# First q norms taken as TensorE columns of squares, and a new order of the first products (attention over channels, then a three-way maxout layer)

## The chip, the cores and the metric

One core of one Trainium2 chip. The metric is the device time of one execution in microseconds (us); a profile of one execution gives the time of every instruction. TensorE is PE in the profile, its weight loads are PEld, VectorE is DVE, ScalarE is ACT, GpSimd is POOL, SyncE is SP.

## The reference, cut to what matters

```python
def _attn_ref(q, k, v, tau):                       # each 4 x 6144 x 256
    qn = q / (np.linalg.norm(q, axis=1, keepdims=True) + 1e-06)
    kn = k / (np.linalg.norm(k, axis=1, keepdims=True) + 1e-06)
    s = kn.transpose(0, 2, 1) @ qn / tau           # 256 x 256 for each batch
    s = s - s.max(-1, keepdims=True)
    a = np.exp(s)
    a /= a.sum(-1, keepdims=True) + 1e-09
    return (v @ a).astype(np.float32)

def _moe_ref(x, w1, w2, w3, w_out):                # x: 24576 x 256, w: 256 x 768
    h = np.maximum(np.maximum(x @ w1, x @ w2), x @ w3)
    return (h @ w_out).astype(np.float32)
```

The kernel multiplies the softmax matrix into the three weights (`aw` = a times w), so that v times `aw` gives h directly. For the first batch nothing can be done before all of q and k are there. Only this first batch is touched by the change; the later ones are prepared beside running work. The tokens of a batch are worked through in chunks of 512, of which chunk 0 and chunk 1 are the first two.

Names in the profile: `gram` is the product of q and k, `e_in` the same after scaling, `et` its exp, `rs_ps` the row sums of `et` and `rinv` their reciprocals; `ew_ps` are the products of `et` with a weight, which are scaled into `aw_sb` (an "evacuation": a copy out of PSUM, the memory that the matmuls write to); `vt` is v transposed. A "piece" of q is what one load brings, 8, 4 or 2 of its 48 groups of 128 tokens.

## The kernel before

The parts that matter, with cuts marked `...`. The q norm comes from the diagonal of q times q, formed beside the gram matrix of q and k:

```python
        for tp in range(NG // 2):
            ...
            for j in range(CC):
                PE.matmul(ps[j][:, 0:C], lhsT=qt[:, tsl, jsl], rhs=kt[:, tsl, :], ...)
                PE.matmul(ps[j][:, C:C + P], lhsT=qt[:, tsl, jsl], rhs=qt[:, tsl, jsl], ...)
    ...
    def softmax_t(ps, rkb):
        for j in range(CC):          # DVE: the diagonal of q*q, by a product with the identity and a sum
            DVE.tensor_tensor_reduce(out=scr, in0=ps[j][:, C:C + P], in1=ident, ...
                                     accum_out=n2q[:, j:j + 1])
        ACT.activation(out=lnq, in_=n2q, func=AF.Ln)
        ACT.activation(out=rq, in_=lnq, func=AF.Exp, scale=-0.5, bias=neg_ln_tau)
        return exp_t(scaled(...), rq)
```

Then six warm-up matmuls, the transposes of the first v on TensorE, and the first part of `aw`: all three weights' products before the first h matmul.

```python
    ps = gram(0)
    for i in range(6):
        PE.matmul(warm_ps, lhsT=ident, rhs=warm, start=(i == 0), stop=(i == 5))
    et = softmax_t(*ps)
    v_transpose_pe(0)
    aw = alloc_aw()
    rinv = aw_first(et, aw)          # products of weights 0, 1, 2; row sums; scaled into aw
    v_transpose(1)                   # by a DMA transpose, for chunk 1
```

## Time and profile before

| what | us |
|---|---|
| time, median of 4 runs (lowest to highest) | 573.54 (573.29 to 574.51) |
| span of the profiled execution | 571.6 |
| last piece of q has landed | 33.75 |
| first exp of the softmax starts | 35.46 |
| first h matmul starts | 37.65 |
| first h matmul of chunk 1 starts | 48.175 |
| transpose of the second v: input landed, result landed | 44.36, 48.07 |

All but the first two rows are moments from the start of the span. A landing is read from the trace's records of a transfer's semaphore: sixteen increments for each transfer (the page counts 16 DMA engines), of which the last is the landing. A "hole" below is a pause of TensorE: the distance between the starts of two matmuls less the pace that matmuls of the size of the first keep when nothing stops them (0.216 us for 512 columns, 0.163 for 384, 0.109 for 256), counted from 0.02 us on.

### The profile page before, as it was taken

What the parts mean: (1) busy time and instruction counts of PE and PEld (TensorE: products, weight loads), DVE (VectorE), ACT (ScalarE), POOL (GpSimd) and SP (SyncE); (2) the same over time, 40 slices, a digit from 0 to 9 for tenths busy, and PEclk for the clock granted to TensorE, in tenths of its full rate; (3) what the DMA queues carried; (4) which work ended last, traced back from release to release, by engine and by line L of the source; (5) the groups of instructions that cost most, each with busy time, mean ns of one, the idle gap of its engine ahead of it and who ended that gap; (6) DMA issues with size and microseconds to landing.
All of it is one profiled execution on the core that took longest, in us unless ns stands there. A gap on an engine that the chain in (4) does not pass through costs nothing.

```text
span 571.6 us, 9437 instructions
## 1 busy us (share of the span) xinstructions
PE 553.2 (97%) x3343; PEld 329.7 (58%) x3344; DVE 416.1 (73%) x658; ACT 309.5 (54%) x540; POOL 233.4 (41%) x237
## 2 busy tenths in 40 slices
PE   3789999999999999999999999999999999999997
PEld 2665555555755555555575555555575555555566
DVE  0048777877887778777767777777768778778775
ACT  1044567677464576776535467767645444444443
POOL 2441357776450078776560058776750000000000
PEclk9999999999999999999999999999999999999999
DMA  9995999884579168884279339984437233132112
GB/s 144 106 172 95 136 239 133 159 134 110 107 86 182 56 116 154 134 150 104 57 131 151 100 81 138 148 141 101 119 86 155 75 78 107 56 104 63 56 55 76
DMA packets 76960, 65.64 MB, mean 115 GB/s; under 512 B 52464, under 2 KB 62576, under 8 KB 76784
## 3 DMA queue, kind: packets, MB, share of 16 engines
q0 software_dynamic: 19072, 26.48, 38.6%
q1 hardware_dynamic: 57696, 38.41, 24.6%
q8 instruction: 26, 0.43, 0.3%
q14 instruction: 22, 0.18, 0.1%
q10 hardware_dynamic: 144, 0.13, 0.1%
HBM read 78.64 MB, written 25.17 MB: 182 GB/s over the span
## 4 chain that ended last, share of the span: by engine, by line
PE 93%; DMA 5%; POOL 0%; issue 0%; DVE 0%; POOLq 0%
PE h_ps L379 65%; PE o_ps L399 22%; DMA q_sb<-in_q_dram 5%; PE gram L250 3%; PE ew_ps L301 3%; POOL k_sb L99 0%; PE o_ps L424 0%; PE ew_ps L325 0%; PE warm_ps L459 0%; PE vt_ps L362 0%; PE gram L181 0%; DVE ht_sb L385 0%; DVE o_sb L451 0%; PE rs_ps L289 0%; PE gram L183 0%
## 5 line engine op out<-in xcount | busy, mean ns | idle before, releaser
L379 PE MATMUL h_ps<-vt_sb,aw_sb 128*128 128x512 bf16 (+1 forms) x1764 | 406.7, 375 | 0.1
L379 PEld LDWEIGHTS <-aw_sb 128*128 128x128 bf16 x1764 | 171.7, 98 | 161.7 <-DVE aw_sb L307 2.4
L384 DVE TENSOR_TENSOR s_mx<-h_ps,s_mx 128x512 bf16<-128x512 f32 (+1 forms) x294 | 198.9, 676 | 82.0 <-ACT s_mx L383 81.8
L383 ACT ACTIVATE s_mx<-h_ps 128x512 bf16<-128x512 f32 (+1 forms) x294 | 172.4, 586 | 124.1 <-PE h_ps L379 123.1
L385 DVE TENSOR_TENSOR ht_sb<-h_ps,s_mx 128x512 bf16<-128x512 f32 (+1 forms) x294 | 200.3, 681 | 30.6
L209 POOL TENSOR_TENSOR acc<-acc,sq 128x768 f32<-128x768 f32 x88 | 144.2, 1648 | 69.3 <-ACT sq L201 53.3
L399 PE MATMUL o_ps<-wo_sb,ht_sb 128*128 128x256 bf16 x1128 | 153.9, 273 | 0.0
L399 PEld LDWEIGHTS <-ht_sb 128*128 128x128 bf16 x1128 | 110.4, 98 | 52.1
L402 ACT ACTIVATE o_sb<-o_ps 128x512 f32<-128x512 f32 x94 | 56.1, 597 | 83.7 <-PE o_ps L399 83.7
L110 POOL DMA_DIRECT2D v_sb<-in_v_dram x48 | 27.8, 584 | 37.6 <-DMA vt_sb<-v_sb 35.4
L201 ACT ACTIVATE sq<-q_sb 128x768 bf16<-128x768 fp8e4 x48 | 40.5, 844 | 0.0
L201 ACT ACTIVATE sq<-k_sb 128x768 bf16<-128x768 fp8e4 x48 | 40.1, 835 | 0.0
L206 POOL CAST acc<-sq 128x768 f32<-128x768 bf16 x6 | 4.9, 820 | 65.0 <-ACT sq L201 65.0
L102 POOL DMA_DIRECT2D q_sb<-in_q_dram x33 | 18.4, 566 | 4.7 <-DMA v_sb<-in_v_dram 3.9
L169 PE MATMUL kk<-k_sb 128*128 128x256 fp8e4 x48 | 7.5, 338 | 11.8 <-DVE k_sb L155 6.4
L99 POOL DMA_DIRECT2D k_sb<-in_k_dram x29 | 16.1, 557 | 2.8 <-issue 1.1
L250 PE MATMUL gram<-k_sb,q_sb 128*128 128x512 fp8e4 x144 | 16.8, 276 | 0.0
L304 ACT ACTIVATE aw_sb<-ew_ps,rinv 128x384 bf16<-128x384 f32 (+1 forms) x24 | 13.2, 555 | 5.7 <-PE ew_ps L301 4.8
L250 PEld LDWEIGHTS <-q_sb 128*128 128x256 fp8e4 x144 | 15.9, 136 | 0.6
L222 POOL PARTITION_ALL_REDUCE tot<-acc x6 | 10.9, 1858 | 11.8 <-issue 5.9
L301 PE MATMUL ew_ps<-w_sb,et 128*128 128x384 bf16 (+1 forms) x96 | 15.6, 313 | 0.0
L181 PE MATMUL gram<-k_sb,q_sb 128*128 128x512 fp8e4 x48 | 11.4, 331 | 2.8 <-DMA q_sb<-in_q_dram 2.7
(64 smaller groups left out, 113.3 us busy)
## 6 DMA issues: line engine op xcount, KB each, us to landing
out_dram<-o_sb SPq DMA_DIRECT2D x41, 512.0 KB, 2.9
v_sb<-in_v_dram POOLq DMA_DIRECT2D x48, 256.0 KB, 4.1
k_sb<-in_k_dram POOLq DMA_DIRECT2D x24, 192.0 KB, 5.7
q_sb<-in_q_dram POOLq DMA_DIRECT2D x24, 192.0 KB, 7.1
out_dram<-o_sb SPq DMA_DIRECT2D x13, 256.0 KB, 2.0
k_sb<-in_k_dram POOLq DMA_DIRECT2D x5, 256.0 KB, 10.7
w_sb<-in_moe_w_dram POOLq DMA_DIRECT2D x9, 128.0 KB, 5.7
kf<-in_k_dram SPq DMA_DIRECT2D x1, 1024.0 KB, 4.9
```

The source lines that it names most:

```text
L102: POOL.dma_start(out=qk[b][0][:, g0:g0 + w, :], in_=q_r[b][:, g0:g0 + w, :])
L110: POOL.dma_start(out=t, in_=v_r[gi // NCH, gi % NCH])
L201: ACT.activation(out=sq, in_=src, func=AF.Square)
L209: POOL.tensor_tensor(out=acc, in0=acc, in1=sq, op=ALU.add)
L250: PE.matmul(g[:, j * C:(j + 1) * C], lhsT=qt[:, tsl, j * P:(j + 1) * P], rhs=kt[:, tsl, :], start=(tp == 0 and j == 0), stop=(tp == NG // ...
L301: PE.matmul(ew[:, :w], lhsT=et[:, j, ic * P:(ic + 1) * P], rhs=w_sb[m][:, j, fsl], start=(j == 0), stop=(j == CC - 1))
L379: PE.matmul(t.rearrange("p (t n) -> p t n", n=P), lhsT=aw[m][:, ic, fsl], rhs=vt[:, tsl, ic, :], start=(ic == 0), stop=(ic == CC - 1))
L383: ACT.activation(out=s_mx, in_=hp[0], func=AF.Copy)
L384: DVE.tensor_tensor(out=s_mx, in0=hp[1], in1=s_mx, op=ALU.max)
L385: DVE.tensor_tensor(out=ht, in0=hp[2], in1=s_mx, op=ALU.max)
L399: PE.matmul(st["ps"][:, half], lhsT=ht[:, fc, t * P:(t + 1) * P], rhs=wo_sb[:, fc, :], start=(fc == 0), stop=(fc == FC - 1))
L402: ACT.activation(out=st["o"][:, t - 1:t + 1, :].rearrange("p t d -> p (t d)"), in_=st["ps"], func=AF.Copy)
```

## The change

Its intent is to shorten the way from the last piece of q to the first h matmul. It has four parts:

1. While the pieces of q arrive, ACT and DVE square them, and TensorE adds the squares of each channel up by matmuls with a single column of ones. The norm is complete four such matmuls after the last square; the two diagonal reductions on DVE go.
2. Two warm-up matmuls in place of six.
3. The transposed first v is written to two banks of PSUM, so that DVE and ACT can copy it at the same time.
4. The third weight's products, and then the first weight's products of the next part, stand between the matmuls of the first h block.

```diff
+        def squares(g0, w):
+            h = w // 2
+            ...
+            ACT.activation(out=a[:, 0:h, :], in_=ra, func=AF.Square)
+            DVE.tensor_tensor(out=d[:, 0:h, :], in0=rd, in1=rd, op=ALU.mult)
+            return [(t, r) for t in (a, d) for r in range(h)]
+        def columns(rows, first=False, last=False):
+            for n, (t, r) in enumerate(rows):
+                for j in range(CC):
+                    PE.matmul(nq[:, j:j + 1], lhsT=t[:, r, j * P:(j + 1) * P], rhs=ones_c, ...)
 ...
-            DVE.tensor_tensor_reduce(out=scr, in0=ps[j][:, C:C + P], in1=ident, scale=1.0, scalar=0.0,
-                                     op0=ALU.mult, op1=ALU.add, accum_out=n2q[:, j:j + 1])
 ...
-    for i in range(6):
-        PE.matmul(warm_ps, lhsT=ident, rhs=warm, start=(i == 0), stop=(i == 5))
+    for i in range(2):
+        PE.matmul(warm_ps, lhsT=ident, rhs=warm, start=(i == 0), stop=(i == 1))
 ...
+        matmuls(0, range(CC))
+        third(lambda: ACT.activation(out=s_mx, in_=hp[0], func=AF.Copy))
+        matmuls(1, range(CC))
+        DVE.tensor_tensor(out=s_mx, in0=hp[1], in1=s_mx, op=ALU.max)
+        aw_part(et, rinv, aw, 1, FT, (0,))
+        matmuls(2, reversed(range(CC)))
+        DVE.tensor_tensor(out=ht, in0=hp[2], in1=s_mx, op=ALU.max)
```

More of the change, by code (lines that the diff above doesn't have):

```diff
@@ L75 @@
     sq_pool = ctx.enter_context(tc.tile_pool(name="sq", bufs=4))
+    sqq_pool = ctx.enter_context(tc.tile_pool(name="sqq", bufs=3))
     sm = ctx.enter_context(tc.tile_pool(name="sm", bufs=2))
@@ L118 @@
     SP.dma_start(out=kf, in_=k_r[0][:, 0:HEAD, :])
-    for load, widths in ((load_k, [8] * 5), (load_q, [8] * 4 + [4, 4, 4, 2, 2])):
+    QW = [8] * 4 + [4, 4, 4, 2, 2]
+    for load, widths in ((load_k, [8] * 5), (load_q, QW)):
         g0 = HEAD if load is load_k else 0
@@ L158, with gram_first @@
     neg_ln_tau = -math.log(float(tau)) if float(tau) != 1.0 else 0.0
-    def gram(b):
-        qt, kt = qk[b]
+    def gram_first():
+        qt, kt = qk[0]
         kk = htile("kk")
@@ L174, in gram @@
             DVE.tensor_tensor(out=dkm[:, jsl], in0=kk[:, jsl], in1=ident, op=ALU.mult)
-        ps = [xtile(f"gram{j}") for j in range(CC)]
-        for tp in range(NG // 2):
-            tsl = slice(2 * tp, 2 * tp + 2)
-            last = tp == NG // 2 - 1
-            for j in range(CC):
-                jsl = slice(j * P, (j + 1) * P)
-                PE.matmul(ps[j][:, 0:C], lhsT=qt[:, tsl, jsl], rhs=kt[:, tsl, :],
-                          start=(tp == 0), stop=last, perf_mode=DR, skip_group_check=True)
-                PE.matmul(ps[j][:, C:C + P], lhsT=qt[:, tsl, jsl], rhs=qt[:, tsl, jsl],
-                          start=False, stop=last, perf_mode=DR, skip_group_check=True)
-            if tp == 11:
+        g = xtile("gram")
+        nq = htile("nq")
+        def squares(g0, w):
+            h = w // 2
+            a = sqq_pool.tile([P, QW[0] // 2, C], BF16, name="sqa")
+            d = sqq_pool.tile([P, QW[0] // 2, C], BF16, name="sqd")
+            ra, rd = qt[:, g0:g0 + h, :], qt[:, g0 + h:g0 + w, :]
+            ACT.activation(out=a[:, 0:h, :], in_=ra, func=AF.Square)
[4 more added lines that the diff above has]
+                for j in range(CC):
+                    PE.matmul(nq[:, j:j + 1], lhsT=t[:, r, j * P:(j + 1) * P], rhs=ones_c,
+                              start=(first and n == 0 and j == 0), stop=(last and n == len(rows) - 1),
+                              skip_group_check=True)
+        g0 = 0
+        rows = None
+        for i, w in enumerate(QW):
+            if rows:
+                columns(rows, first=(i == 1))
+            for tp in range(g0 // 2, (g0 + w) // 2):
+                tsl = slice(2 * tp, 2 * tp + 2)
+                for j in range(CC):
+                    PE.matmul(g[:, j * C:(j + 1) * C], lhsT=qt[:, tsl, j * P:(j + 1) * P], rhs=kt[:, tsl, :],
+                              start=(tp == 0 and j == 0), stop=(tp == NG // 2 - 1), perf_mode=DR,
+                              skip_group_check=True)
+            rows = squares(g0, w)
+            g0 += w
+            if i == 2:
                 kb_ps = htile("kb_ps")
@@ L191, in gram @@
                 ACT.activation(out=rkb, in_=lnk, func=AF.Exp, scale=-0.5)
-        return ps, rkb
+        columns(rows, last=True)
+        return [g[:, j * C:(j + 1) * C] for j in range(CC)], rkb, nq[:, 0:CC]
     SQW = 3
@@ L266, in exp_t, with softmax_first @@
         return et
-    def softmax_t(ps, rkb):
-        n2q = sm.tile([P, CC], FP32, name="n2q")
-        scr = sm.tile([P, P], FP32, name="scr")
-        for j in range(CC):
-            DVE.tensor_tensor_reduce(out=scr, in0=ps[j][:, C:C + P], in1=ident, scale=1.0, scalar=0.0,
-                                     op0=ALU.mult, op1=ALU.add, accum_out=n2q[:, j:j + 1])
+    def softmax_first(gs, rkb, n2q):
         lnq = sm.tile([P, CC], FP32, name="lnq")
@@ L277, in softmax_t @@
         ACT.activation(out=rq, in_=lnq, func=AF.Exp, scale=-0.5, bias=neg_ln_tau)
-        return exp_t(scaled([ps[j][:, 0:C] for j in range(CC)], rkb), rq)
+        return exp_t(scaled(gs, rkb), rq)
     def alloc_aw():
@@ L292, in rowsums, with aw_part @@
         return rinv
-    def aw_part(et, rinv, aw, fp, w):
+    def aw_part(et, rinv, aw, fp, w, ms=range(3)):
         fsl = slice(fp * w, (fp + 1) * w)
         n = 0
-        for m in range(3):
+        for m in ms:
             for ic in range(CC):
@@ L314, in aw_first, with weight @@
         rs_ps = xtile("rs_ps")
-        parts = [(m, ic, htile("ew_ps")) for m in range(3) for ic in range(CC)]
+        parts = []
+        def weight(m):
+            parts.extend((m, ic, htile("ew_ps")) for ic in range(CC))
         def sums(j):
@@ L320, in sums, with products, evacuate, third @@
                           start=(ic == 0 and j == 0), stop=(j == CC - 1), skip_group_check=True)
-        def products(j, ms):
+        def products(j, of):
             for m, ic, ew in parts:
-                if m in ms:
+                if m == of:
                     PE.matmul(ew[:, :FT], lhsT=et[:, j, ic * P:(ic + 1) * P], rhs=w_sb[m][:, j, 0:FT],
                               start=(j == 0), stop=(j == CC - 1))
-        products(0, (0, 1))
+        def evacuate(n, engine):
+            m, ic, ew = parts[n]
+            dst, src, r = aw[m][:, ic, 0:FT], ew[:, :FT], rinv[:, ic:ic + 1]
+            if engine is ACT:
+                ACT.activation(out=dst, in_=src, func=AF.Copy, scale=r)
+            else:
+                DVE.tensor_scalar_mul(out=dst, in0=src, scalar1=r)
+        weight(0)
         sums(0)
+        products(0, 0)
         sums(1)
         DVE.reciprocal(out=rinv, in_=rs_ps[:, 0:CC])
-        products(1, (0, 1))
+        products(1, 0)
+        weight(1)
         for j in range(CC):
-            products(j, (2,))
-        for n, (m, ic, ew) in enumerate(parts):
-            if n % 2 == 0:
-                ACT.activation(out=aw[m][:, ic, 0:FT], in_=ew[:, :FT], func=AF.Copy, scale=rinv[:, ic:ic + 1])
-            else:
-                DVE.tensor_scalar_mul(out=aw[m][:, ic, 0:FT], in0=ew[:, :FT], scalar1=rinv[:, ic:ic + 1])
-        return rinv
+            products(j, 1)
+        for m in range(2):
+            evacuate(CC * m, ACT)
+            evacuate(CC * m + 1, DVE)
+        def third(between):
+            weight(2)
+            for j in range(CC):
+                products(j, 2)
+            evacuate(2 * CC + 1, DVE)
+            between()
+            evacuate(2 * CC, ACT)
+        return rinv, third
     vts = {}
@@ L359, in v_transpose_pe @@
         vt = vt_tile(gi)
-        vt_ps = xtile("vt_ps", cols=TPC * C, dtype=BF16)
-        for i in range(TPC * CC):
-            PE.matmul(vt_ps[:, i * P:(i + 1) * P], lhsT=v_sb[:, i * P:(i + 1) * P], rhs=ident,
-                      is_transpose=True, start=(i == 0), stop=(i == CC * TPC - 1))
-        half = TPC * CC // 2
-        ps = vt_ps.rearrange("p (i n) -> p i n", n=P)
-        DVE.tensor_copy(out=vt[:, half:, :], in_=ps[:, half:, :])
-        ACT.activation(out=vt[:, :half, :], in_=ps[:, :half, :], func=AF.Copy)
+        n = TPC * CC
+        cut = 6
+        banks = [xtile("vt_ps", cols=TPC * C, dtype=BF16), ps_h.tile([P, TPC * C], BF16, tag="h", name="vt_ps2")]
+        for b, (lo, hi) in enumerate(((0, cut), (cut, n))):
+            for i in range(lo, hi):
+                PE.matmul(banks[b][:, i * P:(i + 1) * P], lhsT=v_sb[:, i * P:(i + 1) * P], rhs=ident,
+                          is_transpose=True, start=(i == lo), stop=(i == hi - 1))
+        pa, pb = (t.rearrange("p (i n) -> p i n", n=P) for t in banks)
+        DVE.tensor_copy(out=vt[:, 0:cut, :], in_=pa[:, 0:cut, :])
+        ACT.activation(out=vt[:, cut:n, :], in_=pb[:, cut:n, :], func=AF.Copy)
     def h_block(gi, aw, fc, tsl=slice(0, TPC)):
@@ L384, in h_block, with h_block_first, matmuls @@
         DVE.tensor_tensor(out=s_mx, in0=hp[1], in1=s_mx, op=ALU.max)
+        DVE.tensor_tensor(out=ht, in0=hp[2], in1=s_mx, op=ALU.max)
+    def h_block_first(aw, third):
+        vt = vts[0]
+        hp = []
+        def matmuls(m, ics):
+            t = htile(f"h_ps{m}")
+            for n, ic in enumerate(ics):
+                PE.matmul(t.rearrange("p (t n) -> p t n", n=P), lhsT=aw[m][:, ic, 0:P], rhs=vt[:, :, ic, :],
+                          start=(n == 0), stop=(n == CC - 1))
+            hp.append(t)
+        s_mx = mx_pool.tile([P, CHUNK], BF16, name="s_mx")
+        ht = hts[0][:, 0, :]
+        matmuls(0, range(CC))
[4 more added lines that the diff above has]
+        matmuls(2, reversed(range(CC)))
         DVE.tensor_tensor(out=ht, in0=hp[2], in1=s_mx, op=ALU.max)
@@ L453, in last_chunk @@
         SP.dma_start(out=dst[:, HT + 1, :], in_=o_sb[:, HT + 1, :])
-    ps = gram(0)
+    first = gram_first()
     warm_ps = htile("warm_ps")
-    for i in range(6):
-        PE.matmul(warm_ps, lhsT=ident, rhs=warm, start=(i == 0), stop=(i == 5))
-    et = softmax_t(*ps)
+    for i in range(2):
+        PE.matmul(warm_ps, lhsT=ident, rhs=warm, start=(i == 0), stop=(i == 1))
+    et = softmax_first(*first)
     v_transpose_pe(0)
     aw = alloc_aw()
-    rinv = aw_first(et, aw)
+    rinv, third = aw_first(et, aw)
     v_transpose(1)
@@ L503 @@
                     for fp in range(1, d_ff // FT):
-                        gaps[2 * fp - 2].append(lambda fp=fp: aw_part(et, rinv, aw, fp, FT))
+                        gaps[2 * fp - 2].append(
+                            lambda fp=fp: aw_part(et, rinv, aw, fp, FT, range(1 if fp == 1 else 0, 3)))
                 else:
@@ L532 @@
             for fc in range(FC):
-                h_block(gi, aw, fc)
+                if gi == 0 and fc == 0:
+                    h_block_first(aw, third)
+                else:
+                    h_block(gi, aw, fc)
                 for f in gaps[fc]:
```

## The prediction

> **What bounds the kernel now.** I read the page first: busy shares, slices, then the chain that ended last.
>
> ```profile
> PE 553.2 (97%) x3343; PEld 329.7 (58%) x3344; DVE 416.1 (73%) x658; ACT 309.5 (54%) x540; POOL 233.4 (41%) x237
> ```
>
> TensorE is busy 97% of the span of 571.6 us, and in the 40 slices only the first three and the last are below 9 tenths. So all that a change at the start can win lies before about 48 us, where chunk 1 begins. Next I read the chain in order of time for 30 to 60 us (columns: start, us, what).
>
> ```profile
> 20.81 12.94 DMA q_sb<-in_q_dram
> 33.75 0.04 issue
> 33.80 0.32 PE gram L181
> ...
> 34.41 1.24 PE warm_ps L459 x5
> 35.65 0.45 PE vt_ps L362 x8
> 36.10 0.62 PE ew_ps L325 x4
> ...
> 37.69 1.41 PE h_ps L379 x6
> ```
>
> The first q and k load until 33.75 whatever the engines do; then comes a serial stretch to the first h matmul. From there on TensorE is fed. The warm-up matmuls in the chain only fill time: what the first softmax truly waits for is in the timelines of DVE, ACT and PE (start, us, engine, line, operation, count, idle before):
>
> ```profile
> 34.21 0.29 DVE L272 CUSTOM_DVE_ANT_0 scr<-gram,ident 128x128 f32<-128x128 f32 x1 [14.23 <-PE gram L183]
> 34.99 0.20 ACT L276 ACTIVATE lnq<-n2q 128x2 f32<-128x2 f32 x1 [6.26 <-DVE n2q L272]
> 35.23 0.20 ACT L277 ACTIVATE rq<-lnq 128x2 f32<-128x2 f32 x1
> 35.46 0.91 ACT L265 ACTIVATE et<-e_in,rq 128x256 bf16<-128x256 f32 x2
> 36.56 0.24 PE L319 MATMUL rs_ps<-ones_c,et 128*128 128x1 bf16 x4
> 36.84 0.17 DVE L331 RECIPROCAL rinv<-rs_ps 128x2 f32<-128x2 f32 x1 [0.27 <-PE rs_ps L319]
> 37.65 0.59 PE L379 MATMUL h_ps<-vt_sb,aw_sb 128*128 128x512 bf16 x2
> ```
>
> The reader is to see: 0.75 us of DVE diagonal reductions (34.21 to 34.96) between the last gram matmul and the norms on ACT, then exp, row sums, reciprocal, the evacuation, and the first h at 37.65. Last, what waits at the start of chunk 1 (timeline at 48 us):
>
> ```profile
> 48.11 0.17 PEld L379 LDWEIGHTS <-aw_sb 128*128 128x128 bf16 x2 [0.27 <-DMA vt_sb<-v_sb]
> 48.12 0.19 POOL L470 COPY guard<-vt_sb 128x1 bf16<-128x1 bf16 x1 [10.02 <-DMA vt_sb<-v_sb]
> ```
>
> The weight load for chunk 1 already waits for the DMA transpose of the second v; it comes just in time (matmul 47.96 + 0.216 = 48.175, the next one starts at 48.175, no gap). This is the line that decides the case for me.
>
> **What the Trainium skill says.** (1) "TensorE: Matmul & The Clock Gate", section "Back-to-back issue gap": matmuls of 1 to 64 columns do not go below a start-to-start of about 25 ns. The trace agrees: the four rs_ps matmuls start at 36.559, 36.586, 36.611 and 36.636, each with its own weight load. (2) Same page, "What's actually happening": half clock until a busy window of some 3.4 us. The trace agrees in kind: gram matmuls of 256 columns stand 0.21 us apart until 25.75 and 0.11 after, 5.2 us after TensorE became continuously busy, while the k stage (8 matmuls in each 2.45 us) stayed at half for 14 us. (3) "DMA: Bandwidth & Descriptors", "Where 436 GB/s comes from": a fabric ceiling of 435 GB/s. The trace is near: a q piece of 1 MB of float32 lands every 2.45 us, 428 GB/s (20.53, 22.98, 25.47, 27.90). So loads land at the rate of the queue, and no engine work moves them.
>
> **The change, part by part.**
>
> *Gram stage.* Removed: 48 products of q with itself, 0.055 us each at full clock. Added: 96 column products of one column each. At the 26 ns of the rs_ps row, 16 of them for a piece of 8 cost 0.42 us; removed are 8 x 0.055 = 0.44. TensorE has per piece 8 x 0.111 + 0.42 = 1.3 us of work, at half clock 8 x 0.213 + (0.42 to 0.85) = 2.1 to 2.6, against 2.45 between landings. It keeps up: no change, q still ends at 33.75. Squares beside it: ACT converts 128x1024 in 1.06 us (its k_sb row) and DVE should need about the same, both idle here in the kernel before.
>
> *After the last q.* Before: landing 33.75, gram, two reductions, Ln at 34.99, exp at 35.46, 1.71 us. After: the square of 128x256, some 0.41 us (as the 0.42 of rkb, same size), 33.80 to 34.21; four column products, the last starting 34.37 and ending 0.16 later, 34.54; Ln 34.57, Exp of it 34.81 (the same 0.236 step as before), first exp of the softmax 35.04. Gram of the last piece ends about 34.4 and the two scalings on DVE at 34.86 and 35.2, in time. Gain 0.42.
>
> *Softmax to first h.* Two warm matmuls instead of six let the transposes start when v has landed (34.99). First et visible at 35.6 (was 36.02), second at 36.0; rs_ps at once, reciprocal at 36.25, evacuation at 36.52, h at 37.07 (steps of before: 0.27 from reciprocal to evacuation, 0.55 from there to h). First h 0.58 earlier. The split of vt into two banks lets ACT and DVE copy at the same time; it is off this path. The first two weights' landings (35.62, 36.30) are just met.
>
> *The reorder in the first h block.* The same 36 ew products and 36 h matmuls are done either way; it moves four ew (0.44 us) behind the first h. From the first et to chunk 1 TensorE has 36 x 0.216 + 36 x 0.109 + 0.1 = 11.8 us of work; before it took 48.17 - 36.02 = 12.15, so only 0.35 us of holes are there to be won. After, the holes are: waiting for the second et 0.1, waiting for the first h 0.3 (one weight's products fewer to fill it), 0.1 to 0.15 at seams. TensorE would be through chunk 0 at 35.6 + 11.8 + 0.5 = 47.9, 0.15 to 0.3 us earlier than 48.17.
>
> *Sum.* Loads are issued in the same order and the second v lands from the full queue at 44.36; its transpose lands at 48.07. Chunk 1 cannot start before about 48.12. So of the 0.15 to 0.3 us about 0.05 is left, and the rest becomes a wait of TensorE for vt_sb. From chunk 1 on nothing is changed. Predicted: 573.58 - 0.05, 573.5 us.
>
> **Rivals.** *The wait for vt_sb does not bind* (its transpose lands earlier in an unprofiled or another run): the whole 0.15 to 0.3 is kept, 573.3. Against it: 44.36 follows nine w loads and wo at a steady 0.67 us per w load, a queue without holes. *The column products are dear* : if each pair costs its weight load (98 ns) and not 26 ns, a piece costs 16 x 0.098 + 0.89 = 2.45, TensorE never catches up with what it did not do at half clock, and gram ends up to 3 us later: 574.5 to 576. Against it: the four rs_ps pairs, though four are a short burst. *The clock stays at half*: one-column products may not count as activity, and with warm-up cut from six matmuls to two, h would begin at half clock and lose up to 1.7 to 3 us (half of one or two windows of 3.4 us): 575 to 576.5. For it: the k stage at under half duty never warmed. Against: gram alone streams 1.7 of each 2.45 us, and TensorE has no idle between at half clock. I give each of these two one chance in ten. *ACT or DVE become the bound* in the last pieces (squares of 4 groups 0.6 us each against landings 1.2 apart): they keep up; a slip of 0.2 would be hidden by the same wait.
>
> **Range and chances.** Without the last two rivals: 573.2 to 573.7 plus the spread of three runs (573.29 to 574.51). With them an upper tail to 576. 8 in 10: 572.9 to 574.7. A change of 2% is 11.5 us; nothing here is worth that. Faster 0.01, same 0.98, slower 0.01.
>
> **What would show it right or wrong.** Right: the last q lands at 33.75 as before; first exp of the softmax near 35.0; column products 25 to 30 ns apart at full clock; first h near 37.1; a TensorE idle row of 0.1 to 0.3 us before the h matmul of chunk 1, released by DMA vt_sb, with that matmul at 48.1 to 48.2. Wrong: gram matmuls 0.21 us apart beyond 30 us; TensorE still in gram when the last q has long landed; the first h of chunk 1 later than 48.3, or much earlier than 48.1, which would mean that the transpose was not a floor.

## The result

| | before | changed |
|---|---|---|
| median of 4 runs | 573.54 | 573.17 |
| lowest to highest | 573.29 to 574.51 | 573.01 to 573.62 |
| span of the profiled execution | 571.6 | 571.3 |

The ratio of the changed kernel to the one before is 0.9992, with a 95% interval of 0.9974 to 1.0009. A ratio is the mean time of one kernel's fast runs over that of the other's fast runs of the same rounds, so it is not quite the ratio of the medians. The interval holds 1: by the times alone the kernels are the same, within 2% by far, and 573.17 lies in the range of the prediction (572.9 to 574.7). Everything finer than that is read from the two traces, one execution of each kernel.

The chain of the changed kernel in order of time (start, us, what):

```profile
20.82 12.75 DMA q_sb<-in_q_dram
...
33.67 0.43 ACT sqa L185
...
34.15 0.25 PE nq L192 x4
...
34.48 0.38 PE warm_ps L525
34.85 0.62 PE vt_ps L406 x8
35.47 0.17 PE rs_ps L343 x2
...
36.08 0.18 DVE rinv L364
...
36.36 0.49 DVE aw_sb L358
...
36.88 0.61 PE h_ps L439 x2
```

A chain of this kind steps back along an engine where it finds no waiting, so it has to be read with the timeline. The warm-up is still in it (34.48), and still it only fills time: the transposes behind it wait for the first v, which landed at 34.81, and the last of them starts at 35.25, while the first row sum at 35.44 waits for the first exp, which ends at 35.39. What the first h truly waits for is a square on ACT, four column products, Ln and Exp of the norm, the exp of the softmax, the row sums, the reciprocal and one evacuation.

The timeline of the changed kernel, with the lines that answer to those shown of before (the square brackets have the idle time before an instruction and what ended it):

```profile
34.44 0.17 ACT L296 ACTIVATE lnq<-nq 128x2 f32<-128x2 f32 x1 [0.34 <-PE nq L192]
...
34.64 0.20 ACT L297 ACTIVATE rq<-lnq 128x2 f32<-128x2 f32 x1
...
34.85 0.45 PEld L406 LDWEIGHTS <-v_sb 128*128 128x128 bf16 x8 [0.49 <-DMA v_sb<-in_v_dram]
34.88 0.91 ACT L290 ACTIVATE et<-e_in,rq 128x256 bf16<-128x256 f32 x2
...
35.84 0.11 PEld L343 LDWEIGHTS <-et 128*128 128x128 bf16 x2 [0.23 <-ACT et L290]
...
36.88 0.12 PEld L439 LDWEIGHTS <-aw_sb 128*128 128x128 bf16 x2 [0.40 <-ACT aw_sb L356]
```

Ln of the norm now starts 34.44 - 33.57 = 0.87 us after the last q, where it took 34.99 - 33.75 = 1.24; the first h waits for the evacuation and nothing else. Part 3 did what it is for: the two copies of the transposed v now overlap (35.40 to 36.06 us, where they took from 36.14 to 37.20), but the first h waits for them in neither trace.

| moment, us | before | changed | after the last q, before | after the last q, changed |
|---|---|---|---|---|
| last q landed | 33.75 | 33.57 | 0 | 0 |
| first exp | 35.46 | 34.88 | 1.71 | 1.31 |
| first h matmul | 37.65 | 36.88 | 3.90 | 3.31 |
| first h matmul of chunk 1 | 48.175 | 47.788 | 14.42 | 14.22 |

TensorE reaches chunk 1 0.39 us earlier. Of this 0.18 is only that the last piece of q landed earlier in this execution; 0.21 is the way from there on. The first softmax product comes 1.87 us after the last q, where it came 2.27 after it (35.44 and 36.02 on the clock of the traces): 0.40 gained. The holes of TensorE from there to chunk 1 add up to 0.35 us before and 0.51 now: 0.16 lost. Of the 0.39 us, 0.30 are left at the last matmul of the kernel (567.74 and 567.44); the rest is about what is lost in later holes, which add up to 1.47 us against 1.39 before.

### The profile page after: what moved, and what is told of

Read it like the earlier page. It is cut to its first block, busy times and chain, and to the rows that moved or that the text cites. A ratio compares the mean times of both kernels' runs of the same rounds, so it can differ in the third digit from the quotient of the medians.

```text
span 571.3 us, 9549 instructions
## 1 busy us (share of the span) xinstructions
PE 553.0 (97%) x3387; PEld 328.0 (57%) x3388; DVE 423.2 (74%) x663; ACT 316.3 (55%) x549; POOL 233.7 (41%) x237
## 4 chain that ended last, share of the span: by engine, by line
PE 93%; DMA 5%; POOL 0%; DVE 0%; issue 0%; ACT 0%; ACTq 0%; DVEq 0%; POOLq 0%
PE h_ps L422 65%; PE o_ps L465 22%; DMA q_sb<-in_q_dram 5%; PE gram L275 3%; PE ew_ps L321 3%; POOL k_sb L100 0%; PE o_ps L490 0%; PE h_ps L439 0%; PE ew_ps L349 0%; PE vt_ps L406 0%; DVE aw_sb L358 0%; DVE ht_sb L428 0%; ACT sqa L185 0%; DVE o_sb L517 0%; PE warm_ps L525 0%
## 5 line engine op out<-in xcount | busy, mean ns | idle before, releaser
L185 ACT ACTIVATE sqa<-q_sb 128x1024 bf16<-128x1024 fp8e4 (+2 forms) x9 | 7.0, 773 | 19.2 <-DMA q_sb<-in_q_dram 19.2
L275 PE MATMUL gram<-k_sb,q_sb 128*128 128x512 fp8e4 x144 | 16.8, 276 | 0.0
```

The lines of the kernel that those rows point to most:

```text
L275: PE.matmul(g[:, j * C:(j + 1) * C], lhsT=qt[:, tsl, j * P:(j + 1) * P], rhs=kt[:, tsl, :], start=(tp == 0 and j == 0), stop=(tp == NG // ...
```

## Experiments

No experiment gave a result, so nothing in this section is evidence. Both kernels use the double-row mode of fp8 matmuls.

The kernel before, and the changed kernel, unchanged, in five rounds each, for the spread of their landmarks:

> The kernel before, unchanged, for the spread of its landmarks in the trace. Theory (the loads set their own times, the rest is a fixed chain): from the landing of the last q piece to the first h matmul 3.90 us as in the first trace, to the first h matmul of chunk 1 14.42 us. What I got wrong in the prediction is the DMA transpose of the second v as a floor: it landed 3.71 us after its input in the trace of before, 2.90 in the trace of after. If it is chance, this run may show anything from 2.9 to 3.7; if the kernel decides it, 3.7 again. Time against itself: ratio 1.000 within 0.001.

> The changed kernel, unchanged, with more rounds. Theory: last q to first h 3.31 us, to the first h of chunk 1 14.22 us, so 0.2 us off 573.5, ratio 0.9996; if the whole difference of the medians (0.37 us) is the change, 0.9993; if the 0.4 us was chance alone, 1.000. Transpose of the second v: about 2.9 us if the kernel decides it, anything to 3.7 if it is chance.

The changed kernel with its warm-up put back:

```diff
-    for i in range(2):
-        PE.matmul(warm_ps, lhsT=ident, rhs=warm, start=(i == 0), stop=(i == 1))
+    for i in range(6):
+        PE.matmul(warm_ps, lhsT=ident, rhs=warm, start=(i == 0), stop=(i == 5))
```

> The changed kernel with the six warm-up matmuls of before put back in place of two. Theory (TensorE takes them in order, so the transposes of the first v and all after them stand behind the warm-up): transposes 0.7 us later than in the changed kernel (35.5 instead of 34.85), reciprocal 0.5 to 0.6 later, first h 3.8 to 3.9 us after the last q instead of 3.31, and the start of chunk 1 0.3 to 0.5 later, so the gain of the norms is gone. Rival (the warm-up only fills idle time): no landmark moves.

The norms as columns alone, with the old warm-up, the old copy of v and the old order of the first products:

```diff
-        banks = [xtile("vt_ps", ...), ps_h.tile([P, TPC * C], BF16, tag="h", name="vt_ps2")]
+        vt_ps = xtile("vt_ps", cols=TPC * C, dtype=BF16)
 ...
-    rinv, third = aw_first(et, aw)
+    rinv = aw_first(et, aw)
 ...
-                if gi == 0 and fc == 0:
-                    h_block_first(aw, third)
-                else:
-                    h_block(gi, aw, fc)
+                h_block(gi, aw, fc)
```

> Only the norms as columns of squares; warm-up of six, copy of the transposed v from one bank, and order of the first products as in the kernel before. Theory: the first exp starts 1.3 us after the last q (1.71 before), but the transposes stand behind six warm-up matmuls which now start 0.25 us later after the last q than before, so the first h comes 4.0 to 4.2 us after the last q against 3.90 before: the earlier exp buys nothing alone. Rival (the norm chain was the bound): first h 3.5 us after the last q, 0.4 earlier than before.

In their place stand-ins without the mode were written, with a result that is wrong on purpose:

```diff
-                PE.matmul(g[:, ...], lhsT=qt[:, tsl, ...], rhs=kt[:, tsl, :], ..., perf_mode=DR, ...)
+                PE.matmul(g[:, ...], lhsT=qt[:, 2 * tp, ...], rhs=kt[:, 2 * tp, :], ..., ...)
```

There were stand-ins of the kernel before, of the changed kernel, and of the changed kernel with six warm-up matmuls. They got past that check, but no chip ran any of them, in 18 submissions over some four hours. So the sections below rest on the two traces and on arithmetic from them; what they can't settle is listed as open.

## Why the prediction was right, and where it was not

**The loads: right, with a loose comparison.** A piece of 8 groups landed every 2.43 to 2.49 us in both traces; the last piece came 0.18 us earlier, of which more below. The 428 GB/s that the prediction sets beside the skill's ceiling are counted in float32 as it lies in HBM; what the profile counts there is 105 to 117 GB/s, since q is kept as fp8, a quarter of the size. So the two figures were not shown to be one limit. The argument needs the even steps alone.

**The gram stage: right.** Sixteen column products for a piece of eight were priced at 0.42 us, from four row-sum matmuls. The timeline of TensorE in the changed kernel (start, us, engine, line, operation, count):

```profile
24.80 0.42 PE L192 MATMUL nq<-ones_c,sqa 128*128 128x1 bf16 x8
25.08 0.34 PE L192 MATMUL nq<-ones_c,sqd 128*128 128x1 bf16 x8
25.52 1.09 PE L204 MATMUL gram<-k_sb,q_sb 128*128 128x512 fp8e4 x8
```

Eight column products take 25.08 - 24.80 = 0.28 us with the start of the burst, then 25.2 ns each; a burst of sixteen has the pace that the prediction took from a burst of four. The Trainium skill's floor of about 25 ns ("TensorE: Matmul & The Clock Gate", "Back-to-back issue gap") agrees. TensorE waits for q again between the pieces. The first rival, that a pair costs its weight load of 98 ns, is out.

**The clock: right.** The second rival feared half clock beyond 30 us. The distances of the column products fall from 26.7 to 25.2 ns at 25.03 us, where the record of the granted clock has its step, and gram matmuls of 256 columns stand 0.213 us apart up to 24.58 and 0.109 from 25.68 on. Before, the step was at 25.97. So in these two executions the clock was released no later although a part of the work was one-column matmuls with short pauses; that it was released earlier is no finding from one execution of each. The skill's window of about 3.4 us (same page, "What's actually happening") fits a release 4.5 us after TensorE began on q.

**From the last q to the first exp: right.** 1.29 us were predicted (33.75 to 35.04), 1.31 measured. The square of the last piece took 0.42 us, where 0.41 was estimated. The squares of 1024 elements on DVE were mis-sized: 1.23 us against the 1.06 of ACT, where "about the same" was written. A new piece comes only every 2.45 us, so it cost nothing.

**From there to the first h, and the holes: right.** Predicted 3.32 us after the last q (37.07 - 33.75), measured 3.31. The holes that the reorder leaves were put at 0.5 us in sum, measured 0.51: 0.12 for the second exp, 0.04 for a weight's landing, 0.28 before the first h, 0.07 at the last seam before chunk 1. This explains where 0.59 us of the earlier first h went: 0.44 are the four products moved behind it (4 x 0.109), which have to be done all the same, and the holes after it are smaller by 0.07 (0.07 against 0.14); 0.59 - 0.44 + 0.07 = 0.22, of which 0.21 is seen (holes under 0.02 us aren't counted).

**The wait for the second v: wrong.** "Chunk 1 cannot start before about 48.12", and the rest "becomes a wait of TensorE for vt_sb". The changed kernel has its first h of chunk 1 at 47.788, with no hole before it, and the transpose had long landed:

```profile
47.17 0.19 POOL L536 COPY guard<-vt_sb 128x1 bf16<-128x1 bf16 x1 [9.26 <-DMA vt_sb<-v_sb]
```

GpSimd, which waits for the same transpose, goes on at 47.17 instead of 48.12. The input landed 0.15 us earlier than before (44.21, not 44.36), but above all the transpose took 2.90 us from there (44.21 to 47.11) and not 3.71. Had it taken 3.71 again, it would have landed at 47.92, and chunk 1 could have started at about 47.97, 14.40 us after the last q: nearly all of the 0.21 us would have been lost, as predicted (an estimate from these landings and the 0.05 us from landing to GpSimd's start). The failed step was to take one duration of one transfer as fixed. That it varies stood in the trace of before: its 47 transposes took 2.8 us from issue to landing at least, 3.4 in the median, against 3.7 for this one. What made it long before can be seen in the view of DMA for the stretch from the issue to the landing. First the kernel before (44.3 to 48.1 us; busy tenths of the 16 DMA engines in 40 slices, then queues with packets, MB and share):

```profile
DMA  0000000000600039999990200000899992000000
...
q1 hardware_dynamic: 1056, 0.26, 59.9%
q8 instruction: 1, 0.02, 1.6%
...
vt_sb<-v_sb SPq DMA_TRANSPOSE x1, 3.7
```

And the changed kernel (44.2 to 47.2 us):

```profile
DMA  0000000000000000028999999999995000000000
...
q1 hardware_dynamic: 1056, 0.26, 38.8%
...
vt_sb<-v_sb SPq DMA_TRANSPOSE x1, 2.9
```

The same 1056 packets went in one burst in the changed kernel, and in two bursts with a gap of some 0.6 us between them in the kernel before. In that stretch the only other packet of any queue was one of the queue named "instruction": 16 KB, from 45.25, taking 0.96 us. SyncE's own instruction for this transpose took 2.37 us before and 1.33 now.

One pair of transposes shows little, but the two traces hold 94 of SyncE's. Left out are the 14 issued before 85 us and four that took over 10 us. The other 76, sorted by the packets of the instruction queues ("q8 instruction" moves 16 KB, "q14 instruction" 8 KB) that were under way between issue and landing:

| instruction packets | transposes | issue to landing, us: median | lowest to highest | |
|---|---|---|---|---|
| none | 51 | 3.39 | 2.74 to 4.09 | 45 of them 3.36 to 3.44 |
| of 16 KB | 16 | 4.21 | 3.39 to 5.53 | 14 of them above 3.44 |
| of 8 KB alone | 9 | 4.04 | 2.89 to 4.34 | 8 of them above 3.44 |

The two that met 16 KB and took no longer (3.39 and 3.40) met it in their last 0.5 us. So an instruction packet under way beside a transpose goes with a longer time, by 0.8 us in the median, which is also the difference between 3.71 and 2.90. It is not the only cause: four transposes took 3.75 to 4.09 without one.

**Is that chance, or the change?** The Trainium skill ("Runtime: NRT & Kernel Launch", "Instruction fetch mechanics") says that each engine fetches its instructions over DMA in blocks of 16 KiB, 256 instructions. The traces show TensorE as the owner of the 16 KB packets: there are 26 in each, one for every 254 matmuls and weight loads in the mean, and they come at nearly the same counts in both kernels, not at the same times. The second starts when TensorE has begun 446 of these instructions before and 460 in the changed kernel, the third at 710 and 708, the fourth at 954 and 960. The changed kernel has 88 more of them (3387 + 3388 against 3343 + 3344), all early, which at 6687 / 571.6 = 11.7 instructions per us should bring each later fetch forward by some 7.5 us. The fetch at 45.25 is at 38.85 in the changed kernel, 6.4 us earlier, and the next three are 7.7, 7.2 and 7.6 us earlier. So the added matmuls moved a fetch out of the way of this transpose, a side effect of the change that no one intended. That the fetch is what made the transpose long rests on the table above, not on an experiment; a run with a few added TensorE instructions would have tested it.

**So was the number right for the right reason?** Not quite. The range of 572.9 to 574.7 is 1.8 us wide, so a kernel without any change (573.54) would have lain in it too. The time forecast was 0.05 us below before, as part of a gain of 0.15 to 0.3 us was to be swallowed. The chain gained 0.21, and none of it was swallowed: this is the first of the rivals (573.3), which had been set aside. From 573.58, the time before that the prediction started from, 0.21 less gives 573.37. The measured 573.17 is 0.2 lower still; the earlier landing of q, 0.18, is of this size, but a median of four runs that spread over 0.6 us can't be taken apart so finely. Within the range, the mechanism up to the first h was right to 0.02 us, and the last step was wrong.

**Why q landed 0.18 us earlier.** Fifteen of the sixteen increments of the last piece were there at 32.97 us in both traces. The sixteenth came at 33.75 before and at 33.57 now. From the first piece of q to the fourth the last increment comes 0.16 to 0.21 us after the fifteenth in the kernel before and 0.04 to 0.05 us after it in the changed one. Then an instruction packet of 16 KB is moved (at 29.12 before, at 27.68 now; 0.98 and 0.97 us), and at the end the last increment is 0.79 and 0.60 us late. So the last increment was 0.55 to 0.58 us later after the packet in both, as if one DMA engine lost the time and could not catch up while all are busy. The changed kernel repeats it: its second packet, at 38.85, falls into the same queue of loads, and from the landing at 41.09 on the fifteenth increment is late as well: it comes 0.52 to 0.57 us after the fourteenth, where it was 0.04 to 0.05 from 28 us on; in the kernel before, which has no packet there, this stays at 0.19 to 0.21. The 0.15 us between the kernels were there before, from the k loads on, where the change has nothing to do with it. I take them for chance.

**Open.** Whether the difference in time is more than chance (the interval holds 1). How much each of the four parts gives: the parts were never run apart. In particular, that the earlier exp would be worth little with six warm-up matmuls, because the transposes stand behind them on TensorE, is worked out from their order and was not shown; the trace of before is in keeping with it, as the last transpose starts at 35.88 there and the first softmax product, which waits for the exp, could have followed at 35.94 instead of 36.02, 0.09 us earlier. Whether moving the fetch is what spared the transpose, as told above.

## What to carry to other kernels

Before you claim a gain behind a serial chain, follow the bound engine up to the next fixed event, and not the chain alone: the first h came 0.59 us earlier, but 0.44 of this was work moved behind it, the engine's first softmax product came 0.40 us earlier, its holes after that grew by 0.16, and 0.21 was won. A duration of one transfer is not a floor until you have seen it more than once; look at the spread over all transfers of its kind, and at what else the DMA engines moved in that stretch. Sums over partitions by matmuls with one column cost 25 ns each at full clock here, and here they replaced a diagonal product and its reduction, since the squares could be made on idle engines.

## What the Trainium skill lacked or had wrong

- "Runtime: NRT & Kernel Launch", "Instruction fetch mechanics", calls the cost of a 16 KiB block "mostly hidden". That is said of the engine that fetches; the section has nothing on other data that share the DMA engines. After such a packet of 0.97 to 0.98 us the last of sixteen increments of the q loads came 0.55 to 0.58 us later than it had, on the path that sets the first h, and 16 transposes that met one took 4.21 us in the median, where 51 that met none took 3.39. The page "DMA: Bandwidth & Descriptors" doesn't name fetches among the causes of a late engine.
- "TensorE: Matmul & The Clock Gate", "Back-to-back issue gap", gives the floor of about 25 ns; for a matmul with its own weight load it gives paces at 128 and 512 columns only, and none for one column, nor a floor at half clock. Here one-column products, each with its own load of 128 columns (96 ns in the median), ran 25.2 ns apart within a burst, and 26.7 at half clock.
- The same page, on the release of the clock, has nothing on one-column matmuls. Here a stretch with 16 of them to each 8 matmuls of 256 columns released it after 4.5 us, against 5.4 before (25.97 - 20.57), in one execution of each.
